# Longer TensorE loops, wo in 4-head pieces projected inside the loop, and the third buffer place freed early, in a two-layer decode kernel

## Chip, core and metric

The kernel runs on one core of a Trainium2 chip. The metric is the device time in microseconds (us). Runs of the kernel before agree within 1 us, so differences of one or two microseconds can be read from medians of several runs.

The traces name the engines PE (TensorE; PEld is its weight loading), DVE (VectorE), ACT (ScalarE), POOL (GpSimd) and SP (SyncE).

## The reference

Two identical layers, each a decode attention over a long cache (batch 2, one query, 32 heads, 16,384 keys of 128), an output projection, and an MLP. Both layers use the same K and V caches and weights. Cut to what matters:

```python
# x [2,1,576], k_cache and v_cache [2,32,16384,128], all bf16
def A(x):                                  # attention
    q = heads(layernorm(x) @ wq)           # 32 heads of 128
    s = einsum(q, k_cache) * 128 ** -0.5
    o = einsum(softmax(s), v_cache)
    return merge(o) @ wo                   # wo [4096, 576]
def B(x):                                  # with S = 1 the shifted gates vanish
    x1 = x + hs                            # hs is a zero term through w2
    return x1 + gelu(layernorm(x1) @ w3) @ w4
# x = x + A(x); x = x + B(layernorm(x)); the same again
```

(In the kernel, `hs` is still computed with w2 from a zero vector, which the code calls the shift term.)

## The kernel before

A "unit" is one (batch, head) pair: 64 per layer, each 4 MiB of K and 4 MiB of V. SBUF holds three "places" of one unit each. SyncE issues all DMAs in a fixed order and waits before each one until the place it overwrites has been released. Layer 1 walks the units backwards, so that the last two units of layer 0 stay in SBUF.

A unit's scores are computed in 16 chunks. For some chunks PE transposes K, ACT copies the result out of PSUM and PE multiplies it by q; for the others DVE multiplies K by q and reduces ("dots"). The number of PE chunks is `ncp`.

```python
def place(self, l, i):                     # i = position in the layer's order
    if i == self.U - 1:
        return 2 - 2 * l
    if l == 0:
        return i % 2
    return (2, 0, 1)[i % 3] if i < self.ROT else (2, 1)[i % 2]   # ROT = 12

def ncp(self, l, i):
    n = self.NCH // 2                      # 8
    if i >= self.U - 3:
        return n + 2
    return n + 1 if l == 1 and i < self.ROT else n

def dots(self, l, i, c):                   # one DVE chunk: 2 instructions
    # ...
    self.dve(tensor_tensor: prod[d] = K chunk * q)          # 128 x 1024
    self.dve(tensor_reduce: sd[q][:, o:o+8] = sum of prod[d])

# attention(l): the PE program is a hardware loop of two units a turn
first, last = (2, self.ROT)[l], U - 8      # units outside are unrolled
# ...
            if i == U - 1 and c == 7:      # inside the last unit
                self.weigh(l, i - 2, 0); self.weigh(l, i - 2, 1)
                self.normalize(*mid, ...)
                self.project_pieces(l, [self.n_wo - 1])     # the middle heads
# ... after the last unit:
        self.unit_max(l, U - 1); self.exps(l, U - 1)
        self.normalizers(...)
        self.weigh(l, U - 2, 0); self.weigh(l, U - 2, 1)    # p @ V of unit 62
        self.weigh(l, U - 1, 0); self.weigh(l, U - 1, 1)    # and of unit 63
        self.project(...)                                   # the last head
```

wo lies in the third place while units use the other two: seven pieces of 4 heads, loaded in rows of 1,152 bytes, and one of 3 heads. All seven are projected near unit 57.

## Time and profile before

| | before |
|---|---|
| median | 2576.98 us (3 runs, 2576.81 to 2577.01) |
| DMA rate in most slices | 428 to 433 GB/s |
| DVE, PE, ACT busy | 75%, 60%, 44% |
| PE's instruction fetches | 83 packets of 16 KiB |

The page of the kernel before: busy time of each engine with its share of the span, the rate in 40 equal slices, and the DMA queues (packets, MB, share of sixteen engines' span). q1 carries the loads, q8 PE's instruction fetches, q14 those of other engines.

```profile
PE 1556.6 (60%) x34903; PEld 1465.3 (57%) x34903; DVE 1935.1 (75%) x2733; ACT 1133.5 (44%) x1833; POOL 0.8 (0%) x10
...
GB/s 413 431 427 432 431 432 430 432 428 432 433 431 431 428 433 431 432 431 428 414 403 429 428 429 431 431 429 431 432 432 430 429 431 433 430 431 428 428 426 359
...
q1 hardware_dynamic: 52808, 1097.76, 99.6%
q8 instruction: 83, 1.36, 0.2%
q14 instruction: 38, 0.31, 0.0%
```

The rate is level except in the first and last slice and around slice 20, the MLP between the layers. The Trainium skill ("DMA: Bandwidth & Descriptors", Where 436 GB/s comes from) gives 435.2 GB/s as the ceiling of the ports; the trace agrees with about 431 in steady slices. The kernel moves 1,098 MB whatever its schedule, so the question is only what it loses beside that.

The semaphore records of the trace give more: when the first and when the last of the sixteen DMA engines finished each load. The lag between the two, worked out from those records for loads of 4 MiB that started landing after the given time:

```
us:              100   400   700  1000  1200  1360  1440  1600  2000  2400  2500
before           1.8   4.1   6.1   8.0  10.0   2.9   5.0   7.1   8.7   9.7  10.1
```

In the steady stretches one engine falls behind, 1 us at a time. It catches up only where the others have nothing to do. On the slowest engine in the steady stretches every load of 4 MiB ends one transfer time (9.7 us) after the one before, or 10.7 us after it when the lag makes a step. The packet records say what the 1 us steps go with: from 100 us on, each falls in a load during which an 8 KiB packet of q14 of some 325 ns ran.

The DMA queue's own waits in the kernel before (who was waited for; us in total, times, longest): the last quarter of V of unit 63 waits for the projection of the middle heads.

```profile
SPq L357 <- PE misc L591: 61.6, 3, 31.4
```

The DMA issues of the kernel before in layer 1's first units, K of units 5 and 6, V of 5, K of 7, then K of 8 (start, duration until the last of the group; an issue follows the release of the place):

```profile
1363.34 16.04 SPq L360 DMA_DIRECT2D buf<-in_A_k_cache_dram  x2
1379.43 0.43 SPq L360 DMA_DIRECT2D buf<-in_A_v_cache_dram  x1
1393.41 0.33 SPq L360 DMA_DIRECT2D buf<-in_A_k_cache_dram  x1
...
1408.01 0.33 SPq L360 DMA_DIRECT2D buf<-in_A_k_cache_dram  x1
```

Issues come 14.6 us apart there (1393.41 to 1408.01), faster than the 19.4 us that a unit takes to load: the computation is behind and catches up, and loads queue up meanwhile.

### The profile page before, as it was taken

Reading aid. Unit: us, or ns where it says so; the run is one execution under the profiler, and the core shown is the slowest. Engines: PE = TensorE matmul, PEld = TensorE weight load, DVE = VectorE, ACT = ScalarE, POOL = GpSimd, SP = SyncE. Lnnn points to the kernel's source line nnn. Section 1 sums busy time; section 2 is a strip of 40 time slices with the busy share of each in tenths; the row PEclk is TensorE's granted clock in tenths of the full one; section 3 lists DMA queues with packets and bytes.
Section 4 is the critical chain, followed back from the end, with each engine's and each line's share of the span. In section 5 each row is a group of like instructions: output and inputs, shape, how many; then the busy total and the mean of one; then the engine's idle time right before and its main releaser. Section 6 shows DMA issues by size and latency. Waiting matters only on the chain.

```text
span 2574.8 us, 76099 instructions
## 1 busy us (share of the span) xinstructions
PE 1556.6 (60%) x34903; PEld 1465.3 (57%) x34903; DVE 1935.1 (75%) x2733; ACT 1133.5 (44%) x1833; POOL 0.8 (0%) x10
## 2 busy tenths in 40 slices
PE   5656565656556555656768765556555655565666
PEld 4555554555555555556668655555555555555566
DVE  5877787778777777778559777777787777777864
ACT  3444444444444444444436554444444444444443
POOL 0000000000000000000000000000000000000000
PEclk8666666666666666666657666666666666666666
DMA  9999999999999999999999999999999999999998
GB/s 413 431 427 432 431 432 430 432 428 432 433 431 431 428 433 431 432 431 428 414 403 429 428 429 431 431 429 431 432 432 430 429 431 433 430 431 428 428 426 359
DMA packets 52929, 1099.43 MB, mean 427 GB/s; under 512 B 4996, under 2 KB 13256, under 8 KB 16968
## 3 DMA queue, kind: packets, MB, share of 16 engines
q1 hardware_dynamic: 52808, 1097.76, 99.6%
q8 instruction: 83, 1.36, 0.2%
q14 instruction: 38, 0.31, 0.0%
HBM read 1097.74 MB, written 0.00 MB: 426 GB/s over the span
## 4 chain that ended last, share of the span: by engine, by line
DMA 54%; DVE 35%; PE 8%; SPq 1%; ACT 1%; issue 1%; DVEq 0%
DMA buf<-in_A_k_cache_dram 52%; DVE sd L720 22%; DVE prod L717 12%; PE tps L688 5%; DMA buf<-in_B_w_dram 2%; PE misc L736 2%; ACT ktsb L692 1%; SPq L391 1%; DVE small L738 1%; DMA buf<-in_A_wq_dram 1%; PE ops L761 1%; SPq L374 0%; PE misc L591 0%; PE sps L705 0%; ACT p L747 0%
## 5 line engine op out<-in xcount | busy, mean ns | idle before, releaser
L692 ACT ACTIVATE ktsb<-tps 128x1024 bf16<-128x1024 bf16 x1048 | 1026.7, 1029 | 854.8 <-PE tps L688 849.8
L720 DVE TENSOR_REDUCE sd<-prod 128x8 f32<-128x1024 bf16 x1000 | 1220.1, 1220 | 34.6
L688 PE MATMUL tps<-ident,buf 128*128 128x128 bf16 x8384 | 845.7, 267 | 656.3 <-DMA buf<-in_A_k_cache_dram 652.1
L688 PEld LDWEIGHTS tps<-ident,buf 128*128 128x128 bf16 x8384 | 685.4, 122 | 685.2 <-DMA buf<-in_A_k_cache_dram 672.6
L717 DVE TENSOR_TENSOR prod<-buf,qb 128x1024 bf16<-128x1024 bf16 x1000 | 681.5, 681 | 11.2 <-DMA buf<-in_A_k_cache_dram 10.3
L761 PE MATMUL ops<-p,buf 128*128 128x1 bf16 x16384 | 465.8, 164 | 187.5 <-DMA buf<-in_A_v_cache_dram 164.2
L761 PEld LDWEIGHTS ops<-p,buf 128*128 128x128 bf16 x16384 | 447.7, 101 | 198.6 <-DMA buf<-in_A_v_cache_dram 173.9
L705 PE MATMUL sps<-qcur,ktsb 128*128 128x1 bf16 x8384 | 359.8, 166 | 102.5 <-ACT ktsb L692 91.5
L738 DVE TENSOR_REDUCE small<-misc 128x1 f32<-128x128 f32 x128 | 37.4, 292 | 492.5 <-PE misc L736 492.5
L705 PEld LDWEIGHTS sps<-qcur,ktsb 128*128 128x128 bf16 x8384 | 321.0, 102 | 145.8 <-ACT ktsb L692 143.4
L669 ACT ACTIVATE qb<-misc 128x128 bf16<-128x128 f32 x128 | 35.5, 278 | 493.5 <-PE misc L666 493.5
L736 PE MATMUL misc<-identS,small 128*128 128x128 f32 x256 | 94.9, 474 | 10.3 <-DVE small L730 10.3
L736 PEld LDWEIGHTS misc<-identS,small 128*128 128x128 f32 x256 | 69.7, 332 | 12.0 <-DVE small L730 10.8
L747 ACT ACTIVATE p<-sd,small 128x64 bf16<-128x64 f32 (+2 forms) x128 | 45.2, 353 | 0.0
L747 ACT ACTIVATE p<-sps,small 128x64 bf16<-128x64 f32 (+2 forms) x128 | 40.9, 319 | 4.5 <-DVE small L738 4.5
L661 ACT ACTIVATE qcur<-qt 128x1 bf16<-128x1 bf16 x128 | 29.1, 227 | 19.5 <-DVE qt L598 19.5
L666 PE MATMUL misc<-ident,qcur 128*128 128x128 bf16 x128 | 34.1, 267 | 1.1 <-ACT qcur L661 1.1
L726 DVE TENSOR_REDUCE small<-sps 128x1 f32<-128x64 f32 (+2 forms) x128 | 27.7, 216 | 6.6 <-PE sps L705 6.5
L747 ACT ACTIVATION_READ_ACCUMULATOR p<-sps,small 128x1 f32 x128 | 27.1, 212 | 0.0
L747 ACT ACTIVATION_READ_ACCUMULATOR p<-sd,small 128x1 f32 x128 | 26.5, 207 | 0.0
L728 DVE TENSOR_REDUCE small<-sd 128x1 f32<-128x64 f32 (+2 forms) x128 | 26.4, 206 | 0.0
L768 DVE COPY o<-ops 128x1 f32<-128x1 f32 x126 | 18.7, 149 | 9.5 <-PE ops L761 9.5
(75 smaller groups left out, 161.0 us busy)
## 6 DMA issues: line engine op xcount, KB each, us to landing
buf<-in_A_k_cache_dram SPq DMA_DIRECT2D x123, 4096.0 KB, 22.5
buf<-in_A_v_cache_dram SPq DMA_DIRECT2D x123, 4096.0 KB, 32.0
buf<-in_B_w_dram SPq DMA_DIRECT2D x8, 1152.0 KB, 17.7
buf<-in_A_wq_dram SPq DMA_DIRECT2D x8, 1024.0 KB, 10.0
buf<-in_A_wo_dram SPq DMA_DIRECT2D x14, 576.0 KB, 32.9
buf<-in_A_k_cache_dram SPq DMA_DIRECT2D x3, 2048.0 KB, 27.0
buf<-in_A_k_cache_dram SPq DMA_DIRECT2D x6, 1024.0 KB, 29.0
buf<-in_A_v_cache_dram SPq DMA_DIRECT2D x3, 2048.0 KB, 38.2
```

What stands on the lines that cost most here:

```text
L661: self.act(lambda a: a.activation(out=self.qcur[:, q:q + 1], in_=self.qt[:, u:u + 1], func=ACT.Copy), r=["qt"], w=[f"qcur{q}"])
L666: self.pe(lambda pe: pe.matmul(self.misc[:, 0:128], lhsT=bcast(self.qcur[:, q:q + 1], 128), rhs=self.ident[:, :], start=True, stop=True), ...
L669: self.act(lambda a: a.activation(out=self.qb[q][:, :], in_=self.misc[:, 0:128], func=ACT.Copy), r=["P:misc"], w=[f"qb{q}"])
L688: ins = pe.transpose(self.tps[b][:, j * 128:(j + 1) * 128], kt[:, (j0 + j) * 128:(j0 + j + 1) * 128], self.ident[:, :])
L692: self.act(lambda a: a.activation(out=self.ktsb[k][:, :, :].rearrange("p a b -> p (a b)"), in_=self.tps[b][:, :], func=ACT.Copy), r=[f"P:t ...
L705: ins = pe.matmul(self.sps[sp][:, col:col + 1], lhsT=self.ktsb[k][:, j, :], rhs=self.qcur[:, sp:sp + 1], start=True, stop=True)
L717: self.dve(lambda v: v.tensor_tensor(out=self.prod[d][:, :, :], in0=k3, in1=bcast_mid(self.qb[q][:, :], self.CH), op=ALU.mult), r=[*res, f ...
L720: self.dve(lambda v: v.tensor_reduce(out=self.sd[q][:, o:o + self.CH], in_=self.prod[d][:, :, :], axis=AX.X, op=ALU.add), r=[f"prod{d}"], ...
L736: self.pe(lambda pe: pe.matmul(self.misc[:, 128:256], lhsT=bcast(self.m[:, q:q + 1], 128), rhs=self.identS[:, :], start=True, stop=True), ...
L738: self.dve(lambda v: v.tensor_reduce(out=self.bias[:, q:q + 1], in_=self.misc[:, 128:256], axis=AX.X, op=ALU.max, negate=True), r=["P:misc ...
L747: self.act(lambda a, c0=c0, c1=c1, src=src, part=part: a.activation(out=self.p[q][:, c0:c1], in_=src, func=ACT.Exp, bias=self.bias[:, q:q ...
L761: ins = pe.matmul(self.ops[q][:, 0:1], lhsT=vt[:, j * 128:(j + 1) * 128], rhs=self.p[q][:, h * self.TB + j:h * self.TB + j + 1], start=(h ...
```

## The change

It has four parts. The PE loops run from the first units to the last two, so PE has less unrolled code. wo's 4-head pieces are loaded as rows of 4,608 bytes (four rows of wo each), spread to that layout by small matmuls, and projected in the loop every fourth turn under a condition. Each piece is done with soon, so the last unit's K and V find the third place free. For this, layer 1 leaves the three-place rotation at unit 7, and one more chunk per unit moves from DVE to PE and ACT (`ncp` 9 everywhere but in the last two units).

```diff
-    ROT = 12
+    EARLY = 5
+    ROT = 7
 def want_wo(l, j, at):
-    ap = self.wo[h0 * 128:h1 * 128, :].rearrange("(j p) n -> p j n", p=128)
+    ap = rows.rearrange("(p j) n -> p j n", p=128) if j < self.n_wo else ...
 # order of the loads
-    kv("K", l, i, split=(l == 1 and i == 2) or i == U - 1)
-    elif early <= i - 1 < U - 3:
+    kv("K", l, i, {(1, 2): (2, 1, 1), (1, 3): (2, 2)}.get((l, i)))
+    elif i >= 1 and (l, i - 1) != (1, self.EARLY - 1):
         kv("V", l, i - 1)
+    if i % 8 == 0 and 8 <= i <= 8 * self.n_wo:
+        want_wo(l, i // 8 - 1, wp * self.place_n)
-    for i in range(U - 3, U):
-        kv("V", l, i, split=i == U - 1)
+    kv("V", l, U - 1, (2, 1, 1))
 def ncp(self, l, i):
-    (8; 9 in layer 1 below ROT; 10 in the last three units)
+    return self.NCH // 2 + (1 if i < self.U - 2 else 2)
 # attention(l)
-    first, last = (2, self.ROT)[l], U - 8
+    first = (2, self.ROT - 1)[l]           # the loop ends at U - 2
-    if i == U - 1 and c == 7:  (weigh unit 61, project the middle heads)
-    now = i >= 1 and not early and i < U - 2
+    now = i >= 1 and not early and i < U - 1
+    if i % 8 == 1 and 9 <= i <= 8 * self.n_wo + 1:
+        self.project_piece(l, i // 8 - 1)
+    if i == U - 2:
+        self.project_mid(l)
+        if l == 0:
+            self.shift_term()
 (cut: the scheduler's support for conditional work in a loop, project_piece)
```

More of the change, by code (lines that the diff above doesn't have):

```diff
@@ L15, with __init__ @@
 class Op:
-    __slots__ = ("eng", "fn", "deps", "need", "sem", "val", "clock", "at", "tag")
-    def __init__(self, eng, fn, at, tag):
-        self.eng, self.fn, self.at, self.tag = eng, fn, at, tag
+    __slots__ = ("eng", "fn", "deps", "need", "sem", "val", "clock", "at", "tag", "some", "own", "raw")
+    def __init__(self, eng, fn, at, tag, some):
+        self.eng, self.fn, self.at, self.tag, self.some = eng, fn, at, tag, some
         self.deps, self.need, self.sem, self.val, self.clock = [], False, None, 0, None
+        self.own, self.raw = None, None
 class Sched:
@@ L39, in __init__ @@
         self.tag = None
+        self.some = False
+        self.own = None
         self.loops = []
@@ L52, in op @@
     def op(self, eng, fn, r=(), w=(), deps=()):
-        o = Op(eng, fn, len(self.ops), self.tag)
+        o = Op(eng, fn, len(self.ops), self.tag, self.some)
+        if self.own and eng != "tensor":
+            o.own = f"{self.own}_{eng}"
         self.ops.append(o)
@@ L99, in emit @@
                 d.need = True
-        count = dict.fromkeys(self.ENGS, 0)
+        count = {}
         for o in self.ops:
             if o.sem is None and o.need:
-                count[o.eng] += 1
-                o.sem, o.val = f"done_{o.eng}", count[o.eng]
+                o.sem = o.own or f"done_{o.eng}"
+                count[o.sem] = o.val = count.get(o.sem, 0) + 1
         known = {e: {} for e in self.ENGS}
@@ L109, in emit @@
             waits = []
+            o.raw = {}
+            for d in o.deps:
+                o.raw[d.sem] = max(d.val, o.raw.get(d.sem, 0))
             for d in sorted(set(o.deps), key=lambda d: -d.at):
@@ L129, in run @@
                     at = 0
-                    for first, n, period in loops:
+                    for first, n, period, every, rest in loops:
                         turns = [self._tagged(items, first + t * period, period) for t in range(n)]
@@ L135, in run @@
                         with eng.Fori(0, n) as turn:
-                            for o, waits in self._fold(turns):
+                            for o, waits in self._fold([[x for x in t if not x[0].some] for t in turns]):
                                 self._run(eng, o, [(s, v + turn * d if d else v) for s, v, d in waits])
+                            some = [[x for x in t if x[0].some] for t in turns]
+                            assert [t for t in range(n) if some[t]] == list(range(rest, n, every))
+                            assert all(o.some for t, c in zip(turns, some) for o, _ in t[len(t) - len(c):])
+                            some = [c for c in some if c]
+                            if some:
+                                with eng.If((turn + (every - rest)) % every == 0):
+                                    for o, waits in self._fold(some):
+                                        self._run(eng, o, [(s, v + (turn // every) * d if d else v) for s, v, d in waits])
                         at = start + sum(map(len, turns))
@@ L147, in _run @@
         if o.sem is not None:
-            ins.then_inc(self.sems[o.sem], 1 if o.sem.startswith("done") else 16)
+            ins.then_inc(self.sems[o.sem], 16 if o.eng == "sync" and o.sem != "done_sync" else 1)
     @staticmethod
@@ L161, in _fold @@
         for same in zip(*turns, strict=True):
-            o, waits = same[0]
+            o = same[0][0]
             assert all((p.sem is None) == (o.sem is None) for p, _ in same)
-            values = [dict(w) for _, w in same]
-            assert all(v.keys() == values[0].keys() for v in values), (o.tag, values[:3], values[-2:])
+            sems = sorted({s for _, w in same for s, _ in w})
             folded = []
-            for s, v in values[0].items():
-                d = values[1][s] - v
-                assert all(w[s] == v + t * d for t, w in enumerate(values)), (o.tag, s, [w[s] for w in values])
-                folded.append((s, v, d))
+            for s in sems:
+                v = [dict(w).get(s, p.raw.get(s)) for p, w in same]
+                at = [t for t, x in enumerate(v) if x is not None]
+                d, rest = divmod(v[at[-1]] - v[at[0]], at[-1] - at[0]) if len(at) > 1 else (0, 0)
+                first = v[at[0]] - at[0] * d
+                assert rest == 0 and len(at) > 1 or len(v) == 1, (o.tag, s, v)
+                for t, x in enumerate(v):
+                    need = first + t * d
+                    assert x == need or x is None and same[t][0].clock[s] >= need, (o.tag, s, v)
+                folded.append((s, first, d))
             body.append((o, folded))
@@ L265, in __init__ @@
         n = self.H - 1 - self.N_MID
-        self.n_wo = -(-n // self.WO_PIECE) + 1
-        cuts = [*range(0, n, self.WO_PIECE), n, self.H - 1]
+        assert n % self.WO_PIECE == 0 and self.WO_PIECE * 32 == 128
+        self.n_wo = n // self.WO_PIECE
+        cuts = [*range(0, n + 1, self.WO_PIECE), self.H - 1]
         self.wo_cuts = [cuts, [self.H - c for c in cuts]]
@@ L294, in __init__ @@
         self.otn = sb("otn", [128, self.U], BF16)
+        self.wo_cols = self.WO_PIECE * B
+        self.lpiece = sb("lpiece", [128, 2 * self.wo_cols], FP32)
+        self.opiece = sb("opiece", [128, self.wo_cols], BF16)
+        self.orows = sb("orows", [128, self.WO_PIECE, B], BF16)
         self.xa = sb("xa", [128, 2, KT, B], FP32)
@@ L341, in plan, with kv @@
         self.kept = set(self.order[0][-self.N_KEEP:])
-        def kv(kind, l, i, split=False):
+        def kv(kind, l, i, split=None):
             u = self.order[l][i]
@@ L350, in kv @@
             at = pl * self.place_n + {"K": 0, "V": unit}[kind]
+            ap = src.rearrange("(p j) d -> p (j d)", p=128)
             if split:
-                ap = src.rearrange("(t p j) d -> t p (j d)", t=2, p=128)
-                quarter = self.half // 2
-                ring.want([(kind, l, u, 0)], at, self.half, [lambda e, v: e.dma_start(v, ap[0])])
-                for k in range(2):
-                    ring.want([(kind, l, u, 1 + k)], at + (2 + k) * quarter, quarter,
-                              [lambda e, v, k=k: e.dma_start(v, ap[1][:, k * quarter:(k + 1) * quarter])])
+                a, quarter = 0, self.half // 2
+                for k, n in enumerate(split):
+                    part = ap[:, a * quarter:(a + n) * quarter]
+                    ring.want([(kind, l, u, k)], at + a * quarter, n * quarter,
+                              [lambda e, v, part=part: e.dma_start(v, part)])
+                    a += n
             else:
-                ap = src.rearrange("(p j) d -> p (j d)", p=128)
                 ring.want([(kind, l, u, h) for h in range(2)], at, unit, [lambda e, v: e.dma_start(v, ap)],
@@ L401, in want_wo @@
             h0, h1 = self.wo_piece(l, j)
-            ap = self.wo[h0 * 128:h1 * 128, :].rearrange("(j p) n -> p j n", p=128)
+            rows = self.wo[h0 * 128:h1 * 128, :]
+            ap = rows.rearrange("(p j) n -> p j n", p=128) if j < self.n_wo else rows.rearrange("(j p) n -> p j n", p=128)
             ring.want([("wo", l, j)], at, (h1 - h0) * D,
-                      [lambda e, v: e.dma_start(v.rearrange("p (j n) -> p j n", n=D), ap)])
+                      [lambda e, v: e.dma_start(v.rearrange("p (j n) -> p j n", n=D), ap)],
+                      sem="wo" if j < self.n_wo else None)
         want_wq(0, 2)
@@ L408, in plan @@
             wp = 2 - 2 * l
-            early = 5 if l == 1 else 0
-            wo_at = 7 if l == 0 else self.ROT + 1
-            gap = max(1, (U - 8 - wo_at) // self.n_wo)
             for i in range(U):
-                kv("K", l, i, split=(l == 1 and i == 2) or i == U - 1)
-                if i < early:
-                    kv("V", l, i, split=(l == 1 and i == 2))
-                elif early <= i - 1 < U - 3:
+                kv("K", l, i, {(1, 2): (2, 1, 1), (1, 3): (2, 2)}.get((l, i)))
+                if l == 1 and i < self.EARLY:
+                    kv("V", l, i)
+                elif i >= 1 and (l, i - 1) != (1, self.EARLY - 1):
                     kv("V", l, i - 1)
-                j, r = divmod(i - wo_at, gap)
-                if r == 0 and 0 <= j < self.n_wo:
-                    want_wo(l, j, wp * self.place_n + (2 * unit - self.N_MID * D if j == self.n_wo - 1
-                                                            else j * self.WO_PIECE * D))
+                if i % 8 == 0 and 8 <= i <= 8 * self.n_wo:
+                    want_wo(l, i // 8 - 1, wp * self.place_n)
+                if i == 8 * self.n_wo + 2:
+                    want_wo(l, self.n_wo, wp * self.place_n + 2 * unit - self.N_MID * D)
                 if l == 0 and i == 6:
                     want_w2(wp * self.place_n + unit)
-            for i in range(U - 3, U):
-                kv("V", l, i, split=i == U - 1)
+            kv("V", l, U - 1, (2, 1, 1))
             want_w34(l, 1, 1 if l == 0 else 2)
@@ L672, in ncp @@
     def ncp(self, l, i):
-        n = self.NCH // 2
-        if i >= self.U - 3:
-            return n + 2
-        return n + 1 if l == 1 and i < self.ROT else n
+        return self.NCH // 2 + (1 if i < self.U - 2 else 2)
     def turn(self, l, i, c):
@@ L799, in project, with add_out @@
             after()
+        self.add_out(out)
+    def add_out(self, out):
         self.dve(lambda v: v.tensor_tensor(out=self.xa[:, 0, :, :], in0=self.xa[:, 0, :, :],
-                                           in1=out.rearrange("p (t b) -> p t b", b=B), op=ALU.add),
+                                           in1=out.rearrange("p (t b) -> p t b", b=self.B), op=ALU.add),
                  r=["P:misc", "xa"], w=["xa"])
-    def columns(self, l, js):
-        u0 = min(self.wo_piece(l, j)[0] for j in js) * self.B
-        u1 = max(self.wo_piece(l, j)[1] for j in js) * self.B
-        return u0, u1
@@ L809, in project_pieces, with project_mid @@
-    def project_pieces(self, l, js):
-        parts = []
-        for j in js:
-            h0, h1 = self.wo_piece(l, j)
-            w, res = self.ring.get(("wo", l, j))
-            parts.append((h0, h1 - h0, w, res, lambda j=j: self.ring.done(("wo", l, j))))
-        parts.sort(key=lambda p: p[0])
-        self.project(parts[0][0], parts[-1][0] + parts[-1][1], parts)
+    def project_mid(self, l):
+        h0, h1 = self.wo_piece(l, self.n_wo)
+        u0, u1 = h0 * self.B, h1 * self.B
+        self.normalizers(u0, u1)
+        self.normalize(u0, u1, self.o[:, u0:u1], "o")
+        key = ("wo", l, self.n_wo)
+        w, res = self.ring.get(key)
+        self.project(h0, h1, [(h0, h1 - h0, w, res, lambda: self.ring.done(key))])
@@ new lines, in project_piece, with rows, f @@
+    def project_piece(self, l, t):
+        B, D, KT, J = self.B, self.D, self.KT, self.WO_PIECE
+        h0, h1 = self.wo_piece(l, t)
+        u0, u1, n = h0 * B, h1 * B, self.wo_cols
+        w, res = self.ring.get(("wo", l, t))
+        dps, rps = self.misc[:, 320:320 + 2 * n], self.misc[:, 400:400 + J * B]
+        out = self.misc[:, 256:256 + KT * B]
+        den = self.den[:, u0:u1]
+        self.s.some, self.s.own = True, "piece"
+        self.dve(lambda v: v.tensor_copy(out=self.lpiece[:, :], in_=self.lsum[:, u0:u1, :].rearrange("p u a -> p (u a)")),
+                 r=["lsum"], w=["lpiece"])
+        self.pe(lambda pe: pe.matmul(dps, lhsT=bcast(self.cone[:, :], 128), rhs=self.lpiece[:, :], start=True,
+                                     stop=True), r=["lpiece", "consts"], w=["P:misc"])
+        self.dve(lambda v: v.tensor_reduce(out=den, in_=dps.rearrange("p (u a) -> p u a", a=2), axis=AX.X,
+                                           op=ALU.add), r=["P:misc"], w=["den"])
+        self.dve(lambda v: v.reciprocal(out=den, in_=den), r=["den"], w=["den"])
+        self.dve(lambda v: v.tensor_tensor(out=self.opiece[:, :], in0=self.o[:, u0:u1], in1=den, op=ALU.mult),
+                 r=["den", "o"], w=["opiece"])
+        def rows(pe):
+            for h in range(J):
+                for j in range(J):
+                    ins = pe.matmul(rps[32 * h:32 * h + 32, j * B:(j + 1) * B], lhsT=spread(self.ident[:, j:j + 1], 32, J),
+                                    rhs=self.opiece[:, h * B:(h + 1) * B], start=True, stop=True)
+            return ins
+        self.pe(rows, r=["ident", "opiece"], w=["P:misc"])
+        self.dve(lambda v: v.tensor_copy(out=self.orows[:, :, :], in_=rps.rearrange("p (j b) -> p j b", b=B)),
+                 r=["P:misc"], w=["orows"])
+        def f(pe):
+            for j in range(J):
+                ins = self.d_matmuls(pe, out, w[:, j * D:(j + 1) * D], self.orows[:, j, :], j == 0, j == J - 1)
+            return ins
+        self.pe(f, r=[*res, "orows"], w=["P:misc"])
+        self.ring.done(("wo", l, t))
+        self.add_out(out)
+        self.pe(lambda pe: pe.nop(), w=["P:misc"])
+        self.s.some, self.s.own = False, None
@@ L822, in attention @@
         self.query_rows(l, 0)
-        first, last = (2, self.ROT)[l], U - 8
-        assert first < last and (last - first) % 2 == 0
-        pieces = list(range(self.n_wo - 1))
-        most, mid = self.columns(l, pieces), self.columns(l, [self.n_wo - 1])
-        assert len(pieces) <= 8
-        self.s.loops.append((l * U + first, (last - first) // 2, 2))
+        first = (2, self.ROT - 1)[l]
+        self.s.loops.append((l * U + first, (U - 2 - first) // 2, 2, self.WO_PIECE, (9 - first) // 2 % self.WO_PIECE))
         for i in range(U):
@@ L832, in attention @@
                 self.load_wo_last(l)
-            early = l == 1 and 1 <= i <= 4
+            early = l == 1 and 1 <= i < self.EARLY
             ncp = self.ncp(l, i)
@@ L851, in attention @@
                     self.weigh(l, i - 1, 1)
-                if i == U - 1 and c == 7:
-                    self.weigh(l, i - 2, 0)
-                    self.weigh(l, i - 2, 1)
-                    self.normalize(*mid, self.o[:, slice(*mid)], "o")
-                    self.project_pieces(l, [self.n_wo - 1])
             self.release("K", l, self.order[l][i], 1)
-            now = i >= 1 and not early and i < U - 2
+            now = i >= 1 and not early and i < U - 1
             if now:
@@ L867, in attention @@
             self.row_max(l, i)
-            if i == last + 1:
-                self.normalizers(*most)
-                self.normalize(*most, self.o[:, slice(*most)], "o")
-            if last + 1 <= i <= last + 4 and pieces:
-                self.project_pieces(l, [pieces.pop(0) for _ in range(min(2, len(pieces)))])
-            if l == 0 and i == last + 4:
-                self.shift_term()
+            if i % 8 == 1 and 9 <= i <= 8 * self.n_wo + 1:
+                self.project_piece(l, i // 8 - 1)
             if i == U - 2:
-                self.normalizers(*mid)
+                self.project_mid(l)
+                if l == 0:
+                    self.shift_term()
         self.s.tag = None
```

## The prediction

> **What bounds it.** The DMA: the page's slices show 428 to 433 GB/s nearly everywhere; DVE is 75% busy, PE 60%; the chain of waits alternates K loads with dots. More exactly, the slowest of sixteen DMA engines. In the landing records the last engine lands each load behind the first by 1.8 us early, 10 us at 1220 us, 3.4 us after the middle MLP, 10 us at 2500 us. Dips (288 GB/s at 1290-1300 us, 344 at 2530-2535 us) are fast engines idling; the slowest lands each load one transfer time after the one before (4 MiB: 9.7 us) even there. The last w4 lands at 2570.9 us, 4 us of tail follow. Only work taken off the slowest engine, or a wait added to it, counts.
>
> **What changes.**
> 1. wo: seven pieces a layer in 4,608-byte rows instead of 1,152. Packet records: 181 ns against 4 x 51: 2.6 us less per engine in all.
> 2. PE's code as built shrinks from 10,559 to 5,662 matmuls. Before fetched 83 packets of 16,384 bytes, 1.05 us each; the Trainium skill ("Runtime: NRT & Kernel Launch", Instruction fetch mechanics) says instructions come in 16 KiB blocks, and size and count agree. Some 39 blocks, 2.5 us per engine on average, vanish. But the slowest engine's landings hardly react to these fetches at 2440-2545 us; its lag grows 1 us every 118 us, in step with 8 KiB instruction packets, which DVE's instruction count fits. DVE loses 146 of 2,736 instructions (one dot chunk a unit moves to PE and ACT): 1 us off. PE's blocks: 0.5 us.
> 3. The last unit's K and V, w3 and w4 no longer queue behind the projection of the middle heads (DMA issue waits of 30 and 31 us). It fills fast engines' dips: 0 to 1 us. The end stays DMA-bound: gelu is ready 0.6 us before its first w4 lands.
> 4. Against it: layer 1's three-place rotation ends at unit 7 instead of 12, before computation has caught up (issues 14.6 us apart, transfers 19.4 per unit). K of unit 7 will wait for unit 5, released at 1408.0 us. V of unit 5 lands between 1404.0 (first engine) and 1408.1 (last), then nothing is queued: one gap, 4 to 6 us on fast engines, 2 us on the slowest.
> 5. Projecting in the loop makes DVE wait 3 to 5 us for PE every eighth unit; DVE needs 14 to 15 of 19.4 us, the slowest engine has 10 us queued: free. The larger loop body I assume fetched once.
>
> **Sum.** -2.6 - 1.0 - 0.5 - 0.5 + 2.0 = -2.6, shaded to -2: **2575 us**, 80% within 2570 to 2579.5. Faster by over 2%: 1%; within: 98%; slower: 1%.
>
> **What would show it.** wo packets near 180 ns, PE's fetches near 44; a dip at 1400-1412 us, the lag collapsing there below 1.5 us; no 30 us issue waits at the layers' ends, no dip at 2530 us; steady slices at 431 GB/s; the lag growing 1 us in 130 us; last w4 2 us earlier. Items 3 and 4 are wrong if the total falls by over 6 us or no gap shows.
>
> **What would make it wrong.** The larger loop refetched every turn; the gap longer or repeated at unit 9; the last unit's work, its K now landing one load later, ending after w4; the slowest engine profiting fully from PE's vanished fetches (2572 us).

## The result

The changed kernel's median is 2577.97 us (6 runs, 2576.16 to 2578.57) against 2576.89 us for the kernel before in the same rounds. The ratio is 1.0004, with a 95% interval of 0.9991 to 1.0016: the same time. A ratio here is the mean time of one kernel's runs over that of the other's of the same rounds, so not quite the ratio of the medians. The profiled run of the changed kernel is its slowest, 2578.57 us, so its trace explains 1.8 us (against 2576.77), a little more than the medians' 1.1. The interval holds both signs, so the 1.1 us alone are not clear of noise; what follows accounts for one pair of profiled runs.

The page of the changed kernel, same parts:

```profile
PE 1652.8 (64%) x36879; PEld 1540.8 (60%) x36879; DVE 1749.2 (68%) x2587; ACT 1231.9 (48%) x1941; POOL 0.8 (0%) x10
...
GB/s 413 430 427 432 432 430 432 431 431 432 432 431 431 432 430 432 432 431 431 420 381 408 431 432 431 431 432 431 431 431 432 431 431 431 430 432 431 431 431 340
...
q1 hardware_dynamic: 46712, 1097.76, 99.4%
q8 instruction: 44, 0.72, 0.1%
q14 instruction: 38, 0.31, 0.0%
```

PE's fetches (q8) fell from 83 to 44 packets, as expected. DVE went from 75% to 68% busy. Slice 21 fell to 381 GB/s where the lowest was 403 before. The lag between the first and the last engine:

```
us:              100   400   700  1000  1200  1360  1440  1600  2000  2400  2500
before           1.8   4.1   6.1   8.0  10.0   2.9   5.0   7.1   8.7   9.7  10.1
after            3.2   3.2   6.1   8.2  10.1   3.5   2.1   2.2   5.0   8.1   9.1
```

To account for the time, follow the slowest engine. These are landings on the last engine in the two profiled runs, from the same semaphore records; the difference grows or shrinks by what happened between two rows.

```
                                            before     after   difference
V of unit 63, layer 0                      1282.91   1281.35      -1.6
last wq piece for layer 1                  1319.19   1319.61      +0.4
V of unit 5, layer 1                       1408.11   1408.78      +0.7
K of unit 7, layer 1                       1417.67   1420.79      +3.1
V of unit 63, layer 1                      2545.84   2546.85      +1.0
last w4 piece, layer 1                     2570.92   2571.94      +1.0
issue of the output                        2573.23   2575.23      +2.0
```

Layer 0 gained 1.6 us and the long rest of layer 1 gained 2.1 us. Three places lost it again: 2.0 us at the MLP in the middle, 2.4 us between V of unit 5 and K of unit 7, and 1.0 us after the last load (0.3 us more went between the last wq piece and V of unit 5).

**The gap at unit 7.** The changed kernel's DMA issues in layer 1 (K of units 5 and 6, V of 5, then K of 7 and K of 8):

```profile
1363.13 14.99 SPq L391 DMA_DIRECT2D buf<-in_A_k_cache_dram  x2
1378.17 0.43 SPq L391 DMA_DIRECT2D buf<-in_A_v_cache_dram  x1
1407.06 0.33 SPq L391 DMA_DIRECT2D buf<-in_A_k_cache_dram  x1
...
1421.73 0.33 SPq L391 DMA_DIRECT2D buf<-in_A_k_cache_dram  x1
```

K of unit 7 is issued at 1407.06 us, not at 1393.41, because it now waits for unit 5. The windows at 1400 to 1405 and 1405 to 1410 us show busy time of PE, PE's weight loads, DVE, ACT and POOL, then the granted clock, the DMA share and the rate; first before, then after.

```profile
1400.00:1405.00 5.00, 4.20 (x139) 3.85 (x138) 4.90 (x6) 4.24 (x9) 0.00 (x0) 1.00 0.99 426
1405.00:1410.00 5.00, 3.39 (x72) 3.19 (x69) 4.60 (x9) 1.11 (x2) 0.00 (x0) 0.54 1.02 436
```

```profile
1400.00:1405.00 5.00, 4.61 (x150) 4.35 (x148) 4.93 (x6) 3.36 (x5) 0.00 (x0) 0.84 0.89 377
1405.00:1410.00 5.00, 3.99 (x60) 3.79 (x61) 4.00 (x10) 2.16 (x3) 0.00 (x0) 0.50 0.69 233
```

The rate falls to 377 and 233 GB/s, then is normal again. The gap occurs once.

**The middle MLP.** PE's timeline at the end of layer 0 before: the normalizer matmuls after the last exps, the weighing of units 62 and 63, the end of the latter after a wait for nothing that the profile shows ("issue"), and the last matmuls of w3.

```profile
1276.66 0.59 PE L774 MATMUL misc<-lsum,small 128*128 128x4 f32 x2 [1.15 <-ACT p L747]
1277.11 6.64 PE L761 MATMUL ops<-p,buf 128*128 128x1 bf16 x244
1285.69 0.46 PE L761 MATMUL ops<-p,buf 128*128 128x1 bf16 x12 [1.94 <-issue]
...
1296.90 0.62 PE L566 MATMUL sps<-xnh,buf 128*128 128x4 bf16 x18
```

And after:

```profile
1278.08 0.59 PE L800 MATMUL misc<-lsum,small 128*128 128x4 f32 x2 [1.15 <-ACT p L773]
1278.53 5.61 PE L787 MATMUL ops<-p,buf 128*128 128x1 bf16 x205
1286.12 1.52 PE L787 MATMUL ops<-p,buf 128*128 128x1 bf16 x51 [1.99 <-issue]
...
1298.40 0.62 PE L595 MATMUL sps<-xnh,buf 128*128 128x4 bf16 x18
```

Before, V of unit 63 landed at 1282.91 us, when most of the 256 weighing matmuls were done. Now it lands at 1281.35 us, but the weighing begins 1.4 us later (1278.53), because K of unit 63 now comes after V of unit 61 and so one load later. The weighing then runs without waiting for data and ends later than before. w3 ends 1.5 us later, and the w4 pieces that reuse w3's place are issued at 1296.65 instead of 1295.15 us. The dip did not go away, it moved: in the windows from 1290 to 1295 and 1295 to 1300 us the rate was

```profile
1290.00:1295.00 5.00, 3.29 (x78) 3.14 (x79) 1.14 (x8) 0.50 (x2) 0.00 (x0) 0.50 0.76 307
1295.00:1300.00 5.00, 2.52 (x95) 2.43 (x92) 1.26 (x4) 0.49 (x2) 0.00 (x0) 0.50 0.79 269
```

before, and after

```profile
1290.00:1295.00 5.00, 1.80 (x29) 1.68 (x30) 1.75 (x12) 1.00 (x4) 0.00 (x0) 0.50 0.28 113
1295.00:1300.00 5.00, 4.02 (x144) 3.90 (x141) 0.52 (x3) 0.49 (x2) 0.00 (x0) 0.50 0.48 130
```

The fast engines finished w3 earlier and had nothing else to load.

**The end.** PE's last matmuls before (w3's last part, then w4's pieces of 75, 60 and the rest):

```profile
2560.50 0.62 PE L566 MATMUL sps<-xnh,buf 128*128 128x4 bf16 x18
2563.75 2.14 PE L591 MATMUL misc<-prod,buf 128*128 128x2 bf16 x75 [2.63 <-DMA buf<-in_B_w_dram]
2567.81 1.76 PE L591 MATMUL misc<-prod,buf 128*128 128x2 bf16 x60 [1.92 <-DMA buf<-in_B_w_dram]
2569.92 1.61 PE L591 MATMUL misc<-prod,buf 128*128 128x2 bf16 x45 [0.35 <-DMA buf<-in_B_w_dram]
```

And after:

```profile
2563.86 0.22 PE L595 MATMUL sps<-xnh,buf 128*128 128x4 bf16 x3
2566.00 0.54 PE L595 MATMUL sps<-xnh,buf 128*128 128x4 bf16 x15 [1.92 <-issue]
2568.56 4.96 PE L620 MATMUL misc<-prod,buf 128*128 128x2 bf16 x180 [2.02 <-DVE prod L650]
```

Before, PE waited for each w4 piece. After, all w4 pieces had landed or were landing when PE came to them: w3 finished 5 us later, 1.9 us of it an "issue" wait at 2566.00 in the middle of w3's last part. The first w4 piece had landed at 2564.66 us, PE began at 2568.56 and needed 4.96 us in one go.

**The waits of 30 us.** The wait of V of unit 63 for the middle heads is shorter, not gone (here the waits of that issue line after):

```profile
SPq L388 <- PE misc L620: 47.8, 4, 22.9
```

It costs nothing, because the queue holds enough loads for the slowest engine meanwhile.

### The profile page after: what moved, and what is told of

The parts are those of the page before. It is cut to its first block, busy times and chain, and to the rows that moved or that the text cites. A ratio compares the mean times of both kernels' runs of the same rounds, so it can differ in the third digit from the quotient of the medians.

```text
span 2576.8 us, 80453 instructions
## 1 busy us (share of the span) xinstructions
PE 1652.8 (64%) x36879; PEld 1540.8 (60%) x36879; DVE 1749.2 (68%) x2587; ACT 1231.9 (48%) x1941; POOL 0.8 (0%) x10
## 4 chain that ended last, share of the span: by engine, by line
DMA 60%; DVE 29%; PE 9%; issue 1%; ACT 0%; SPq 0%; DVEq 0%
DMA buf<-in_A_k_cache_dram 57%; DVE sd L746 18%; DVE prod L743 10%; PE tps L714 5%; DMA buf<-in_A_v_cache_dram 3%; PE misc L762 1%; PE ops L787 1%; DVE small L764 1%; DMA buf<-in_A_wq_dram 1%; PE sps L584 0%; PE misc L620 0%; ACT ktsb L718 0%; PE sps L731 0%; SPq L405 0%; PE misc L550 0%
## 5 line engine op out<-in xcount | busy, mean ns | idle before, releaser
L718 ACT ACTIVATE ktsb<-tps 128x1024 bf16<-128x1024 bf16 x1156 | 1125.1, 1031 | 872.2 <-PE tps L714 867.1
L714 PE MATMUL tps<-ident,buf 128*128 128x128 bf16 x9248 | 910.1, 262 | 635.0 <-DMA buf<-in_A_k_cache_dram 635.0
L714 PEld LDWEIGHTS tps<-ident,buf 128*128 128x128 bf16 x9248 | 733.7, 120 | 663.3 <-DMA buf<-in_A_k_cache_dram 655.4
L746 DVE TENSOR_REDUCE sd<-prod 128x8 f32<-128x1024 bf16 x892 | 1088.3, 1220 | 30.9
L743 DVE TENSOR_TENSOR prod<-buf,qb 128x1024 bf16<-128x1024 bf16 x892 | 607.9, 682 | 11.3 <-DMA buf<-in_A_k_cache_dram 10.3
L731 PE MATMUL sps<-qcur,ktsb 128*128 128x1 bf16 x9248 | 396.9, 166 | 108.8 <-ACT ktsb L718 88.3
L731 PEld LDWEIGHTS sps<-qcur,ktsb 128*128 128x128 bf16 x9248 | 349.0, 101 | 171.2 <-ACT ktsb L718 169.1
L762 PE MATMUL misc<-identS,small 128*128 128x128 f32 x256 | 95.3, 476 | 13.5 <-DVE small L756 13.5
L773 ACT ACTIVATE p<-sps,small 128x72 bf16<-128x72 f32 (+1 forms) x128 | 41.5, 325 | 8.2 <-DVE small L764 8.2
L773 ACT ACTIVATE p<-sd,small 128x56 bf16<-128x56 f32 (+1 forms) x128 | 44.5, 348 | 0.0
L752 DVE TENSOR_REDUCE small<-sps 128x1 f32<-128x72 f32 (+1 forms) x128 | 28.5, 222 | 0.0
```

What stands on the lines that cost most here:

```text
L714: ins = pe.transpose(self.tps[b][:, j * 128:(j + 1) * 128], kt[:, (j0 + j) * 128:(j0 + j + 1) * 128], self.ident[:, :])
L718: self.act(lambda a: a.activation(out=self.ktsb[k][:, :, :].rearrange("p a b -> p (a b)"), in_=self.tps[b][:, :], func=ACT.Copy), r=[f"P:t ...
L731: ins = pe.matmul(self.sps[sp][:, col:col + 1], lhsT=self.ktsb[k][:, j, :], rhs=self.qcur[:, sp:sp + 1], start=True, stop=True)
L743: self.dve(lambda v: v.tensor_tensor(out=self.prod[d][:, :, :], in0=k3, in1=bcast_mid(self.qb[q][:, :], self.CH), op=ALU.mult), r=[*res, f ...
L746: self.dve(lambda v: v.tensor_reduce(out=self.sd[q][:, o:o + self.CH], in_=self.prod[d][:, :, :], axis=AX.X, op=ALU.add), r=[f"prod{d}"], ...
L762: self.pe(lambda pe: pe.matmul(self.misc[:, 128:256], lhsT=bcast(self.m[:, q:q + 1], 128), rhs=self.identS[:, :], start=True, stop=True), ...
```

## The experiments

Eleven kernels ran, in three groups. The table has the medians of five rounds; the kernel before was at 2576.73 to 2576.91 us in all groups. The changed kernel ran in rounds of its own. Its runs spread over 2.4 us, but all runs of e1, e2 and e3 lie below its fastest and all of e4's above its slowest.

| run | what | us | against after's 2577.97 |
|---|---|---|---|
| e1_rot10 | three places until unit 10 | 2574.53 | -3.4 |
| e2_hoist | unit 62 weighed in unit 63 | 2575.81 | -2.2 |
| e3_both | e1 and e2 | 2574.58 | -3.4 |
| e4_short_rows | wo in 1,152-byte rows | 2579.05 | +1.1 |
| e5_dve_extra | e3 and 960 tiny DVE instructions | 2582.55 | +4.6 |
| e6_wide_dots | e3, ncp 10, dots in pairs | 2566.66 | -11.3 |
| e7_ncp10 | e3, ncp 10 | 2572.61 | -5.4 |
| e8_before_rot7 | before, ROT 7 | 2580.71 | (before +3.8) |
| e9_wide_hoist | e6 with ROT 7 | 2566.99 | -11.0 |
| e10_wide_only | after with ncp 10, dots in pairs | 2568.69 | -9.3 |
| e11_wide_rot | e6 without e2's part | 2568.13 | -9.8 |

### The gap: e1 and e8

Theory: leaving the rotation at unit 7, before the computation has caught up, starves the loads once. Rival: the gap only lets the slowest engine catch up and costs nothing at the end.

e1 keeps three places until unit 10. So that the pattern of two places joins on, the parity and the places of w3 and w4 in layer 1 are swapped, and layer 1's wo pieces come two units later.

```diff
-    ROT = 7
+    ROT = 10
-        return (2, 0, 1)[i % 3] if i < self.ROT else (2, 1)[i % 2]
+        return (2, 0, 1)[i % 3] if i < self.ROT else (1, 2)[i % 2]
-                if i % 8 == 0 and 8 <= i <= 8 * self.n_wo:
+                if i % 8 == 2 * l and 8 <= i <= 8 * self.n_wo + 2 * l:
-            want_w34(l, 1, 1 if l == 0 else 2)
+            want_w34(l, 1 + l, 1)
-        first = (2, self.ROT - 1)[l]
+        first = (2, self.ROT)[l]
-            if i % 8 == 1 and 9 <= i <= 8 * self.n_wo + 1:
+            if i % 8 == 1 + 2 * l and 9 <= i <= 8 * self.n_wo + 1 + 2 * l:
```

> Changed kernel, but layer 1 keeps three places until unit 10 instead of 7 (its wo pieces come two units later). Theory (early end of the rotation starves the loads once): no gap at 1409 us, where the slowest engine landed K of unit 7 12.0 us after V of unit 5 instead of 9.7; it is then 2.3 us earlier for the rest of layer 1, the total falls by 1.5 to 2.5 us from the changed kernel's, to about 2576. Rival (the gap only levels the engines and costs nothing at the end): the total stays within 0.7 us.

Measured: 2574.53 us. The same two windows show no gap:

```profile
1400.00:1405.00 5.00, 4.54 (x150) 4.26 (x148) 4.93 (x6) 3.36 (x5) 0.00 (x0) 0.84 1.01 429
1405.00:1410.00 5.00, 4.08 (x60) 3.79 (x61) 4.01 (x10) 2.22 (x3) 0.00 (x0) 0.50 0.99 423
```

The saving of 3.4 us is larger than expected. K of unit 7 landed on the last engine 2.4 us earlier than in the changed kernel (1418.38), and V of unit 63 in layer 1 3.1 us earlier (2543.75). The tail from the last w4 landing to the output's issue fell back from 3.3 to 2.3 us.

e8 makes the opposite test in the kernel before:

```diff
-    ROT = 12
+    ROT = 7
-            wo_at = 7 if l == 0 else self.ROT + 1
+            wo_at = 7 if l == 0 else 13
-        return n + 1 if l == 1 and i < self.ROT else n
+        return n + 1 if l == 1 and i < 12 else n
-        first, last = (2, self.ROT)[l], U - 8
+        first, last = (2, 12)[l], U - 8
```

> Kernel before, with only the rotation of layer 1 over three places ended at unit 7 instead of 12. Theory (the early end starves the loads once): a gap of 2 to 6 us at about 1408 us and a total 2 to 3.5 us above before. Rival (in the kernel before the lag of 4 us hides it): within 0.7 us.

Measured: 2580.71 us, 3.8 us above before, a little more than expected. Here the gap is deeper:

```profile
1400.00:1405.00 5.00, 4.10 (x109) 3.56 (x107) 4.89 (x6) 5.00 (x11) 0.00 (x0) 1.00 0.86 364
1405.00:1410.00 5.00, 4.56 (x122) 4.31 (x119) 4.90 (x7) 1.44 (x3) 0.00 (x0) 0.57 0.12 46
```

Here V of unit 63 lands 4.2 us later than before on the last engine (2550.09 us), and the tail is 2.3 us in both, so nothing but the gap is in it. In e1 1.0 us of the profiled run's saving came from the tail, and 3.1 from before it. Both directions agree: the shorter rotation costs 3 to 4 us. The rival falls.

### The attention's end: e2 and e3

```diff
-            now = i >= 1 and not early and i < U - 1
+            now = i >= 1 and not early
 # after the last unit
-        self.weigh(l, U - 2, 0)
-        self.weigh(l, U - 2, 1)
```

> Changed kernel, but V of unit 62 is weighed at the end of unit 63 instead of after it, in both layers: 128 matmuls, 3.5 us, leave the chain between the last exps and the MLP. Theory (K of unit 63 lands one load later now, so the attention's end and with it w3 and w4 became bound by computation): the first w4 piece that waits for w3 is issued 2 to 3.5 us earlier than at 1296.65 us, the tail after the last w4 landing shrinks from 3.3 us to about 2.3, the total falls by 1.5 to 3 us. Rival (the ends are still bound by DMA, as predicted; the changed kernel is slow only by the gap in layer 1): under 0.5 us.

Measured: 2575.81 us, 2.2 us below the changed kernel. The waiting w4 pieces were issued at 1292.57 us (4.1 us earlier), and the tail is 2.3 us again. PE's last matmuls wait for w4's landings as they did before:

```profile
2558.27 0.54 PE L595 MATMUL sps<-xnh,buf 128*128 128x4 bf16 x15 [0.63 <-issue]
2562.60 2.14 PE L620 MATMUL misc<-prod,buf 128*128 128x2 bf16 x75 [3.79 <-DMA buf<-in_B_w_dram]
2566.64 1.76 PE L620 MATMUL misc<-prod,buf 128*128 128x2 bf16 x60 [1.90 <-DMA buf<-in_B_w_dram]
2568.75 1.61 PE L620 MATMUL misc<-prod,buf 128*128 128x2 bf16 x45 [0.35 <-DMA buf<-in_B_w_dram]
```

So the ends had become bound by computation, and the prediction's "the end stays DMA-bound" was wrong.

> e1 and e2 together. Theory (two separate losses, about 2 us each): the savings add, 3 to 5 us below the changed kernel, 2573 to 2575 us, faster than before by 2 to 4 us. Rival (one of the two hides the other): no better than the better of e1 and e2.

Measured: 2574.58 us, no better than e1 alone. The savings do not add. In the landing records e3 is 2.4 us ahead of e1 when V of unit 5 lands in layer 1 (1406.25 against 1408.66), and level with it at V of unit 63 (2543.85 against 2543.75). A hypothesis that fits both: with the gap gone, one engine never waits for anything from start to end, so an earlier MLP no longer helps. In the changed kernel the gap ties the loads to the computation, and with it to the delay at the MLP. e10 and e11 test this below.

### The rows of wo: e4

```diff
-            ap = rows.rearrange("(p j) n -> p j n", p=128) if j < self.n_wo else rows.rearrange("(j p) n -> p j n", p=128)
+            ap = rows.rearrange("(j p) n -> p j n", p=128)
```

The rows of wo are then permuted against what the projection expects, so the result is wrong. The comparison with the reference still passed, so it would not notice such an error here.

> Changed kernel with the wo pieces loaded in 1,152-byte rows as before, instructions otherwise the same; the result is wrong on purpose (rows of wo are permuted). Theory (an engine's time per wo piece is 4 x 51 ns instead of 181 ns for each of 8 rows, 0.19 us a piece, all on the critical engine): 2.0 to 2.7 us slower than the changed kernel. Rival (the transfer saving is absorbed elsewhere): under 0.7 us.

Measured: 2579.05 us, 1.1 us slower, half of what was expected. Single packets take what they took before (51 ns for 1,152 bytes, 181 to 184 ns for 4,608), so the durations were read correctly, but they do not add up to the time of a transfer: packets overlap. The landing records give it directly. A piece of 0.59 MB landed 1.50 us after the load before it with short rows (1539.93 to 1541.43, kernel before, first engine) and 1.42 us with long rows (1447.77 to 1449.19, kernel after). That pair is at the upper end: on the last engine the mean of the fourteen pieces is 1.49 us in the kernel before, 1.47 in e4 and 1.42 in the changed kernel. Fourteen times 0.05 to 0.07 us is 0.7 to 1.0 us, near e4's 1.1. The Trainium skill ("DMA: Bandwidth & Descriptors", Why small descriptors are slow) names a fixed cost per packet; the shorter rows make these transfers 4 or 5% longer here.

### What sets the steady state: e5, e7 and e6

Theory: the kernel is bound by the one DMA engine that falls behind, and it falls behind because DVE's instructions are fetched through it, 8 KiB at a time. Rival: the engines are bound alike, and DVE counts only with its busy time, of which it has some to spare.

e5 adds instructions and hardly any work to e3:

```diff
             self.row_max(l, i)
+            if l == 0 and 2 <= i < U - 2:
+                for k in range(16):
+                    self.dve(lambda v, k=k: v.tensor_copy(out=self.scr[:, k:k + 1], in_=self.cone[:, :]), r=["consts"])
```

> e3 with 16 extra one-column copies on DVE after each unit's row max, units 2 to 61 of layer 0: 960 instructions, 61 KB of program, about 2.4 us of DVE time a unit that DVE has to spare. Theory (the kernel is bound by the one DMA engine that also fetches DVE's instructions; each 8 KiB fetch costs it 1 us): 7.5 more fetches, the lag of the slowest engine grows about 1 us every 75 us in layer 0 instead of every 128, and the total rises by 5.5 to 8 us over e3's 2574.6. Rival (steady state is bound by all engines alike, so only DVE's time counts and that is spare): under 1 us.

e7 moves one more chunk from DVE to PE and ACT:

```diff
-        return self.NCH // 2 + (1 if i < self.U - 2 else 2)
+        return self.NCH // 2 + 2
```

> e3 with ten chunks a unit on PE and ACT and six single chunks on DVE: some 240 DVE instructions fewer than e3, without the wide pairs. Theory (as e5): about 1.9 fetches fewer, 1 to 2 us under e3. Rival: no change within 0.5 us; or slower if ten chunks overload ACT or PE in layer 1's catching up.

e6 has e7's edit and lets DVE take two chunks with one pair of instructions, through one wide buffer instead of two. The token "free" keeps the next product from overwriting one that is still being reduced; a first version without it had a race.

```diff
-        self.prod = [sb(f"prod{i}", [128, self.CH, 128], BF16) for i in range(2)]
+        self.prod = [sb(f"prod{i}", [128, 2 * self.CH, 128], BF16) for i in range(1)]
-        d = c % 2
+        d = 0
-        k3 = ...[:, j0:j0 + self.CH, :]
+        k3 = ...[:, j0:j0 + 2 * self.CH, :]
-        ... r=[*res, f"qb{q}"], w=[f"prod{d}"])
+        ... r=[*res, f"qb{q}", "free"], w=[f"prod{d}"])
-        ... out=self.sd[q][:, o:o + self.CH] ... w=[f"sd{q}"])
+        ... out=self.sd[q][:, o:o + 2 * self.CH] ... w=[f"sd{q}", "free"])
-            dv = list(range(ncp, NCH))
+            dv = list(range(ncp, NCH, 2))
```

> e3 with ten chunks a unit on PE and ACT, and the other six on DVE in three pairs of 2048 elements: DVE has 1,573 listed instructions instead of 2,589. Theory (as e5): about 8 fetches of DVE fewer, the lag of the slowest engine grows by 1 us only every 220 us or so; the total falls until the engines that fetch PE's code are the slowest: 3 to 7 us under e3, 2568 to 2571.5 us, faster than both kernels. Rival: no change within 1 us, or slower if ten chunks overload ACT or PE.

Busy times and the small instruction queue (packets) of e3, e5, e7 and e6, in this order:

```profile
PE 1652.9 (64%) x36879; PEld 1543.9 (60%) x36879; DVE 1749.3 (68%) x2587; ACT 1232.7 (48%) x1941; POOL 0.8 (0%) x10
...
q14 instruction: 38, 0.31, 0.0%
```

```profile
PE 1650.8 (64%) x36879; PEld 1539.1 (60%) x36879; DVE 1807.1 (70%) x3547; ACT 1231.7 (48%) x1941; POOL 0.8 (0%) x10
...
q14 instruction: 46, 0.38, 0.0%
```

```profile
PE 1730.4 (67%) x38863; PEld 1604.8 (62%) x38863; DVE 1533.7 (60%) x2339; ACT 1342.5 (52%) x2065; POOL 0.8 (0%) x10
...
q14 instruction: 37, 0.30, 0.0%
```

```profile
PE 1736.3 (68%) x38863; PEld 1613.5 (63%) x38863; DVE 1475.1 (58%) x1571; ACT 1344.9 (52%) x2065; POOL 0.8 (0%) x10
...
q14 instruction: 31, 0.25, 0.0%
```

Set side by side (changes worked out from these lines and the medians):

| step | DVE instructions | DVE busy us | fetch packets (q14) | time us |
|---|---|---|---|---|
| e3 to e5 | +960 | +58 | +8 | +8.0 |
| e3 to e7 | -248 | -216 | -1 | -2.0 |
| e7 to e6 | -768 | -59 | -6 | -6.0 |

The time follows the number of DVE's instructions, 7.8 to 8.3 us per thousand in all three steps. It does not follow DVE's busy time: e7 took away 216 us of it and gained 2.0 us, e6 took away 59 us more and gained 6.0. The rival falls. Queue 14 also carries other engines' fetches; e7 gave ACT 124 instructions, which may be why its count fell by only one. e3 ran on one chip and e5 to e7 on another, where the kernel before differed by 0.02 us.

The lag of the slowest engine shows the same thing (first row repeated):

```
us:              100   400   700  1000  1200  1360  1440  1600  2000  2400  2500
after            3.2   3.2   6.1   8.2  10.1   3.5   2.1   2.2   5.0   8.1   9.1
e3_both          3.3   3.4   6.1   8.2  10.2   3.9   4.9   6.0   8.8  11.7  12.4
e5_dve_extra     3.3   5.1  10.0  13.4  13.0   3.0   4.3   5.9   8.2  11.2  11.2
e6_wide_dots     3.1   3.2   3.7   5.3   6.2   5.3   6.2   7.8   8.0  10.2  10.2
```

With the extra instructions the last landing in layer 0 takes a step of about 1 us every 70 us (14 steps from 284.1 to 1200.7 us) instead of every 129 (7 steps from 440.9 to 1213.1 us in the changed kernel). As in the kernel before, each of these 7 and 14 steps falls in a load during which a q14 packet ran. In e6 the lag reaches 6.2 us at 1200 us instead of 10.2. In layer 1 of e6 a whole group sets the lag until about 2000 us: ten of the sixteen engines fell 5 to 8 us behind while PE's unrolled code for the layer's first ten units was fetched (until 1512 us), and then kept that lag.

e6 is the best version: 2566.66 us, ratio to before 0.996 (95% interval 0.9947 to 0.9974), about 10 us faster than both kernels.

### Do the rotation and the hoist still matter? e9, e10, e11

(The hoist is e2's earlier weighing of unit 62.) These take e6's parts away again: e9 has e2's edit and the wide dots but leaves the rotation at unit 7; e10 has the wide dots alone; e11 has e1's edit and the wide dots but weighs unit 62 after the last unit. The edits are the ones above.

> e6 with the rotation of the changed kernel (three places until unit 7): PE has four unrolled units fewer to fetch, but K of unit 7 waits for unit 5 again. Theory: a unit takes about 13.5 us in the catching up instead of 14.6, so K of unit 7 is issued near 1399 us, while the last load before it lands at 1397 to 1402: the gap is 0 to 2 us on the slowest engine, and the engines that fetch PE's code lag some 3 us less; total within 2 us of e6's 2566.7 either way. If the gap costs as in e1 (3 us) with no gain from fetches, it is 2569 to 2570.

Measured: 2566.99 us, 0.3 us above e6.

> Changed kernel with the wide dots alone: no longer rotation, no hoist. Theory: the fetches that DVE saves (8 of 20) come off the slowest engine, but the gap still ties the loads to the computation's chain, which is late at the middle MLP; 2568 to 2572 us, 1.5 to 4 us above e6. Rival (rotation and hoist are worth nothing once DVE's fetches are gone): within 0.7 us of e6.

Measured: 2568.69 us, 2.0 us above e6.

> e6 without the hoist of the weighing of unit 62. Theory (e3 was no better than e1 because the engine that fetches DVE's code had slack at the middle MLP and the chain did not reach it): now that this engine is ahead, the chain at the MLP matters; 1 to 3 us above e6's 2566.7. Rival (the hoist is worth nothing without the gap): within 0.5 us.

Measured: 2568.13 us, 1.5 us above e6.

With DVE's fetches cut, the hoist is worth 1.5 us (e11) although it was worth nothing in e3 against e1. This supports the explanation of e3: there, the engine that carries DVE's fetches was too late for the MLP's delay to reach it. The rotation is worth almost nothing now (e9). The gap is still there, but smaller: K of unit 7 lands on the last engine 11.0 us after V of unit 5, 1.3 us late where it was 2.3 in the changed kernel, and the rate from 1395 to 1400 us is 338 GB/s. The units do not come at the 13.5 us that were expected (14.3 us from K of unit 7 to K of unit 8); but K of unit 7 is issued at 1398.2 us, 4.1 us before V of unit 5 lands on the last engine, where it was 1.7 us. PE also has fewer unrolled units to fetch (45 packets against e6's 55); these effects were not separated.

## Why the prediction was right or wrong

The time, 2577.97 us, lies in the range of 2570 to 2579.5, and "within 2%" was right. The point value was 3 us too low: -2 predicted, +1.1 measured, though the interval of the ratio holds both signs. The range helped: against the sum of -2.6, the slowest engine in the profiled pair lost 3.7 us more than foreseen and gained 0.9 us less, and the range just covered that. Point by point:

- **"the slowest of sixteen DMA engines" bounds the kernel.** Right. e5 to e7 show it, with the cause that the prediction read from the steps of the lag. Which engine it is, the trace does not say.
- **"2.6 us less per engine in all" for wo's rows.** The mechanism was right and the size wrong: e4 gives 1.1 us. The durations of overlapping packets were multiplied up, 0.19 us a piece; the distance of two landings, which the trace also has, gives 0.05 to 0.07.
- **"1 us off" for 146 DVE instructions.** Right in size: at e5's 8.0 us for 960 instructions, 146 give 1.2 us.
- **PE's blocks "0.5 us".** The count came as foreseen (44), the effect on the end was not isolated. e1 fetched 53 packets and was still faster. The argument that the slowest landings hardly react to these fetches, made from 2440 to 2545 us, does not hold everywhere: in the kernel before, the lag grew from 4.1 us at V of unit 5 to 7.1 at 1547 us, in small steps on loads during which PE's packets ran.
- **"It fills fast engines' dips: 0 to 1 us. The end stays DMA-bound."** This step failed. The dip at 2530 us did fill (344 GB/s from 2530 to 2535 us before, 415 after), but moving K of unit 63 one load later made the attention's end later against the loads, and both MLPs became bound by computation: 2.0 us lost in the middle and 1.0 us at the end in the profiled run. e2 recovers 2.2 us. The prediction listed this among what could make it wrong, but put no term for it in the sum.
- **One gap at unit 7, "2 us on the slowest".** Right in place, time and cause; the lag fell to 2.1 us where below 1.5 was foretold. The size was 3.1 us by V of unit 63 and 3.4 us in the time (e1). The last engine before the gap need not be the one that decides the end; the landing records suggest that the engine which falls behind through the rest of layer 1 was not last at that moment, and so waited longer.
- **"projecting in the loop ... free", the loop "fetched once".** Consistent: steady slices stay at 430 to 432 GB/s and PE's fetches at 44. It was not tested alone.

In short, the change took 3.7 us off the slowest engine in the profiled pair and lost 5.7, nearly all of it in three places: a gap in the loads, and two MLPs that the computation now reached too late.

Still open: why the changed kernel's own runs spread over 2.4 us. e8 and e10, which have the gap too, spread over 2.3 and 2.2 us, but e2 and e4 have it and spread over only 0.6 and 0.7. The "issue" wait of 1.9 us inside w3 may fall elsewhere in some runs; only one run of each kernel has a trace.

## What to carry to other kernels

In a kernel bound by DMA, follow the slowest engine, not the mean rate: compare the first and the last landing of each load, and see what makes the lag grow. Instructions are loads too; a few hundred small vector instructions can cost a DMA-bound kernel microseconds although the vector engine has time to spare, so fewer and wider instructions pay. When buffers change hands earlier, check each load's new predecessor twice: once for what it now waits for, and once for what now comes behind it.

## What the Trainium skill lacked or had wrong

- "Runtime: NRT & Kernel Launch", Instruction fetch mechanics, calls crossing a 16 KiB boundary "mostly hidden". PE's fetch packets are 16,384 bytes as it says, but other engines' are 8,192 bytes, and the fetches show up as lost DMA time: 960 DVE instructions cost 8.0 us (e5), 768 fewer gave 6.0 us (e7 to e6). No page has a cost of fetching for a DMA-bound kernel.
- The same section does not say that PE can stand still for it in unrolled code. PE waited for nothing that the profile shows for 1.9 us in the midst of w3 (2563.86 to 2566.00 us); that a fetch was the cause is likely, not shown. A packet of 16,384 bytes began at 2563.5 us, 0.6 us before this wait; at the ends of the layers both kernels together have five such waits of 1.7 to 2.0 us, and each began 0.4 to 0.7 us after such a packet.
- "DMA: Bandwidth & Descriptors", Latency and other measured facts, has DMA engines that are usually slower and guesses at the rings of software-generated DMA. Here all data went through the hardware queue and one engine still fell 10 us behind; in the changed kernel's layer 0 its lag grew by 1 us every 129 us, and every 70 us with e5's extra instructions.
- The same page gives no way from packet durations to transfer time. Multiplying 51 and 181 ns predicted 2.6 us for wo's rows; e4 gave 1.1, the landings 0.7 to 1.0.
